# Value matmuls in blocks of eight key tiles instead of four, in a planned attention and feed-forward kernel

## The chip, the cores and the metric

The kernel runs on one core of a Trainium2 chip. The metric is the device time of one execution in microseconds, as the median of several runs. TensorE is called PE here, ScalarE ACT, VectorE DVE, GpSimd POOL and SyncE SP, as the profile does; PEld is PE's weight load.

## The reference

A layer norm without scale, then multi-query attention and a gated feed-forward block beside each other, all in fp32. The sequence has 2048 rows of width 448; there are 16 heads of width 28 that share one key and one value head; the feed-forward width is 1792.

```python
xn = _layernorm(x)
q = (xn @ wq).reshape(B, S, 16, 28).transpose(0, 2, 1, 3)
k, v = xn @ wk, xn @ wv
p = softmax(einsum("bhqd,bkd->bhqk", q, k) * 28 ** -0.5)
attn = einsum("bhqk,bkd->bhqd", p, v).transpose(0, 2, 1, 3).reshape(B, S, 448) @ wo
mlp = (silu(xn @ w1) * (xn @ w3)) @ w2
out = x + attn + mlp
```

## The kernel before

The 2048 query rows are taken in four chunks of 512 (`NQ`). A chunk of one head is called a head here: there are 64 (`NH`), numbered `h`, each against 16 key tiles of 128 rows (`KT`).

The work of a head:

- *Leads* (`leads`, matmul at L792, tile `ld`): the scores of all 16 key tiles, one 512-column matmul each. DVE takes the running maximum over them (`mx`, L803). ACT copies those of the key tiles that are kept, in neighbouring pairs, from PSUM to SBUF (`pa`, L797): five pairs for some heads (`TEN`), six for every second head from the twelfth on (`TWELVE`).
- The maximum over the keys, negated, is written to DRAM (`md`) and comes back as one row of the query stack (`qs`) and as a broadcast tile (`mb`).
- *Weights* (`weights_of`): for a kept pair POOL adds `mb` (L839, 128x1024) and ACT takes the exponential (L841). For the other tiles PE computes the score again, with the maximum as an extra row of the contraction (`sc`, L846), and ACT takes the exponential from PSUM (`pb`, L849).
- *Values* (`values`, L866): one matmul per key tile and head, with the 128x32 value tile as weights (28 columns, one column of ones for the sum of the softmax, padding) and the 128x512 exponentials as the moving operand, in plain fp32. Its output goes to one of four 32-column strips: the head's parity and the position's parity choose it. Each such matmul is two instructions.
- `pair_done` moves the sums of two heads from the bank `av` to `o` (ACT L881, DVE L882); after four heads `norm` divides and splits (POOL L914 and L918), and `out_project` multiplies with `wo`.

The values are issued in blocks. A block is one operation of the plan: it waits for all exponentials that it needs and issues its matmuls one after another. It takes `AVK` positions of head h (the first half of its order) and `AVK` positions of head h-1 (the second half):

```python
for i in range(AVK):
    for g, n in ((h, AVK * j + i), (h - 1, KT // 2 + AVK * j + i)):
        if 0 <= g < NH:
            todo.append((avb[g // 2], g, n, *pt[g, kept(g)[2][n]]))
...
cost = AVK / 2 * 858.0 + 300.0
plan.base = begin(h) + T * AVK * (j + 1) / KT + 1.5
```

The caller runs `j` over `range(KT // AVK // 2)`. With `AVK = 4` that is two blocks per head step of at most eight matmuls; h goes from 0 to 64, so there are 130 blocks, those of the first and the last step with one head only.

Beside this runs the feed-forward part (`hidden`): for each of 56 pieces (four chunks by 14) the chains `g` and `u` of 11 matmuls each (`gate_up`), a tanh on ACT (L686), two products on DVE (L688, L694), and a split into a high and a low part, ACT (L698) and POOL (L700, tile `h`); then `down`, chains `dn` whose results DVE adds to `acc` (L723). All matmuls of these chains and of the projections are written by `chain` (L409). In the first chunk the weights are loaded raw and split by ACT and POOL (L650, L652, L666, L668), stored, and reloaded for the later chunks. At the start come the norm, transposes (`xp`, L541) and the projections `q`.

The order on every engine is fixed when the program is built. `Plan.order` simulates the five engines with a cost for each operation and always issues the ready one with the lowest due time on each engine. The due times are made of `T0`, `T`, `LEAD`, `SPAN` (heads), `MDUE`, `MSTEP`, `MEND` (feed-forward), `XDUE`, `QDUE`, `QSTEP`, `XSTORE` (start, projections, stores) and a shift per kind of operation (`PUT`: engine and the buffers touched). An operation that needs new buffers is held back by `SOON` (how far ahead of PE's next due time it may go), `MOST` and `SPARE` (how many buffers a kind may hold, how many it must leave). Buffers come from three pools: single tiles of 2 KB per partition (`PAGES`, 18), double ones (`PAIRS`, 39) and the eight banks of PSUM. All DMAs are issued by SP. The value tiles use pairs (`pa`) and pages (`pb`).

Of the kernel before, what the change touches and what calls it, by code (L numbers as in the profile page):

```python
# [40 lines left out]
TWELVE = ((1, 4, 6, 9, 11, 14), (1, 0, 3, 2, 4, 5, 6, 7, 8, 9, 10, 11, 12, 13, 14, 15),  # L41
          (1, 2, 4, 5, 0, 6, 7, 9, 10, 3, 11, 12, 14, 15, 8, 13))
FROM, OF, MANY = 12, 2, 1
AVK = 4
T0, T, LEAD, SPAN = 73.28, 32.63, 14.04, 29.75
XDUE = (4.15, 8.15, 12.15, 16.15)
QDUE, QSTEP = 21.57, 6.09
SINGLE = 2
XSTORE = 22.5, 16.1
MDUE, MRUSH, MSTEP = 40, 11, 10.34  # L50
MEND = 7.58
RATE = 18.1
QUEUES = 16
LANES = 8
BACKLOG = 1565.91
LATE = 901.2
HLV = 0
EARLY = 16
BULK = ("w13", "w2", "x", "raw", "raw2", "acc")
SOON = {"pa": 30.2, "qs": 15.3, "acc": 15.9, "o": 18.3, "x": 24.2}  # L60

PUT = {"ACT ": -1.32, "ACT at pa": 0.93, "ACT at pb": -0.15, "ACT at x": 1.75, "ACT at xp": 8.68,
        "ACT av o": -9.5, "ACT h mi": -0.39, "ACT h t": -0.01, "ACT kv qp": -3.95, "ACT lb o oh": -0.08,
        "ACT mi t": -0.59, "ACT mi x": 2.0, "ACT o oh": 1.81, "ACT qp qt": -0.15, "ACT raw w13": -16.73,
        "ACT raw wo": 7.09, "DVE ": 1.37, "DVE acc": -5.45, "DVE acc xn": -2.36, "DVE at m": -0.89,
# [11 lines left out]
PAIRS = 39  # L77
PAGES = 96 - 2 * PAIRS
SLACK = 5.49
REST = 70.26  # L80
LOADING = 60
BANKS = 8
MOST = {"pa": 33, "x": 25, "acc": 10, "w13": 9, "w2": 8, "h": 3, "oh": 12, "wo": 4, "xt": 3, "xn": 1, "wq": 14,
        "qt": 4, "pb": 12, "raw": 4, "raw2": 5, "t": 2, "qs": 5, "m": 4, "mxt": 7, "mb": 7, "o": 19, "lb": 7,
        "xp": 33, "wr": 8, "kv": 7, "at": 5, "mi": 21, "av": 9, "qp": 14}
SPARE = {"x": 2, "acc": 4, "w13": 2, "w2": 4, "raw": 2, "raw2": 2, "qt": 6, "wo": 1, "qs": 2}


class Buf:
# [24 lines left out]
class Plan:  # L114
# [10 lines left out]
    def op(self, eng, cost, fn, reads=(), writes=(), parts=(), prio=0.0, after=(), lat=None, size=0, also=(), behind=None, k=16, port=False):  # L125
# [17 lines left out]
        o.bufs = list({id(b): b for b in bufs if b.ap is None}.values())  # L143
        o.prio += PUT.get(eng + " " + " ".join(sorted({b.cat for b in o.bufs})), 0.0)
        for b in o.bufs:
# [11 lines left out]
    def order(self):  # L157
        import heapq
        pools = list(range(PAGES)), list(range(PAIRS)), list(range(BANKS))
        pages, pairs, banks = pools  # L160
        used = dict.fromkeys(MOST, 0)
        ready = {e: [] for e in self.ENGINES}
# [13 lines left out]
        def head():  # L176

            while line and line[0][1] in issued:
                heapq.heappop(line)
            return line[0][0] if line else 1e9  # L180

        def can(o, early=False):
# [9 lines left out]
            if early:  # L192
                if any(len(p) - k < EARLY for k, p in zip(need[:2], pools) if k):
                    return False
            elif any(o.prio > head() + SOON.get(c, 40.0) for c in cats):
                return False
            if any(k > len(p) for k, p in zip(need, pools)):
                return False
            for c, k in cats.items():
                if used[c] + k > MOST[c] or len(pools[kinds[c]]) - need[kinds[c]] < SPARE.get(c, 0):  # L200
                    return False
# [16 lines left out]
        while todo:  # L218
            progress = True
            while progress:  # L220
                progress = False
                for e in self.ENGINES:
# [3 lines left out]
                    for o in ready[e]:  # L226
                        if best is not None and (o.prio, o.n) >= (best.prio, best.n):
                            continue
                        if e == "SP" and max(queues) - now > BACKLOG and o.prio > 40.0 and o.bufs and any(b.cat in BULK for b in o.bufs):
                            continue  # L230
# [114 lines left out]
def build(ctx, tc, x, wq, wk, wv, wo, w1, w3, w2, out):  # L345
# [208 lines left out]
    def x_store(qc):  # L554
        scr[qc] = dr.tile([7, P, TC], F32, tag=f"scr{qc}", name=f"scr{qc}")
        sbuf = fixed(scr[qc])
        store_ops[qc] = sbuf
        for c in range(7):
            b = xs[qc][c]
            dma(P * TC * 4, lambda b=b, c=c: nc.sync.dma_start(scr[qc][c], f32(b.ap)), reads=[b], parts=[sbuf])  # L560
# [34 lines left out]
    for qc in range(NQ):  # L595
        plan.base = XDUE[qc]
        norm_and_split(qc)
# [12 lines left out]
    for qc in range(1, NQ):  # L610
        plan.base = XSTORE[0] + XSTORE[1] * qc
        x_store(qc)
# [122 lines left out]
    def due(i):  # L735
# [3 lines left out]
        t = MDUE + MSTEP * MRUSH  # L739
        return t + (T0 + T * (NH + 1) / 2 + MEND - t) * (i - MRUSH) / (NQ * NF - MRUSH)  # L740

# [24 lines left out]
    def begin(h):  # L766

        return T0 + T / 2 * h
# [83 lines left out]
    def values(h, j):  # L852


        todo = []
# [7 lines left out]
        def fn():  # L863
            for a, g, n, p, i in todo:
                r = 64 * (n % 2) + 32 * (g % 2)
                nc.tensor.matmul(a.ap[r:r + 32], vst_ap[:, kept(g)[2][n]], p.ap if i is None else p.ap[:, i], start=(n < 2), stop=(n >= KT - 2),  # L866
                                 skip_group_check=True)
        cost = AVK / 2 * 858.0 + 300.0
        plan.base = begin(h) + T * AVK * (j + 1) / KT + 1.5
        av_last[0] = plan.op("PE", cost, fn, lat=cost + 160.0,  # L870
# [98 lines left out]
    for qc in range(NQ):  # L969
# [4 lines left out]
        for h in range(16 * qc, 16 * qc + (17 if qc == NQ - 1 else 16)):  # L974
            if h < NH:
                stack_load(h)
                leads(h)
            for j in range(KT // AVK // 2):
                for i in range(AVK * j, AVK * (j + 1)):
                    if h < NH:  # L980
# [17 lines left out]


# [17 lines left out]
```

## Time and profile before

| what | value |
|---|---|
| runs | 1123.69, 1124.69, 1121.7 us; median 1123.69 |
| profiled execution, first to last instruction (span) | 1120.7 us |
| PE busy | 1104.6 us, 5758 matmul instructions |
| PE weight loads busy | 736.5 us |
| POOL busy | 994.1 us, 499 instructions |
| ACT busy | 982.9 us, 1628 instructions |
| DVE busy | 946.0 us, 1802 instructions |
| DMA | 168.66 MB, 150 GB/s mean |
| mean granted TensorE clock | 0.997 |

The profiled execution is known by its span alone, so its own time is that span and what lies around it; the runs' times are 1.0 to 4.0 us above the span. Busy time of an engine is the union of its instructions' times. A matmul's row is longer than the distance to the next one, since matmuls are pipelined; the distance from start to start tells PE's pace. Rows of the timeline join neighbouring instructions of one kind (x3), with the start of the first.

### The profile page before, as it was taken

How to read it: one execution, taken by the hardware profiler on the slowest of the kernel's cores; microseconds unless marked ns; L12 is line 12 of the kernel's file. 1: busy time of each engine (PE TensorE's matmuls, PEld its weight loads, DVE VectorE, ACT ScalarE, POOL GpSimd, SP SyncE). 2: the span in 40 equal slices, each digit the busy share in tenths (PEclk: the TensorE clock that was granted, in tenths of full speed). 3: DMA queues.
4: the chain of work that ended last, by engine and by line, in shares of the span. 5: the costliest groups of instructions: out<-in, count | busy, mean ns of one | idle time of the engine just before them, and what ended most of it. 6: DMA issues, size and time to landing. Idle time of an engine off the chain costs nothing.

```text
span 1120.7 us, 18422 instructions
## 1 busy us (share of the span) xinstructions
PE 1104.6 (99%) x5758; PEld 736.5 (66%) x5758; DVE 946.0 (84%) x1802; ACT 982.9 (88%) x1628; POOL 994.1 (89%) x499
## 2 busy tenths in 40 slices
PE   6999999999999999999999999999999999999998
PEld 4877667666666676666666666666666676667664
DVE  7879776898898989899899888899889889898834
ACT  3466888999999989999899999999899989998962
POOL 3226999999999998999999998999989999999983
PEclk9999999999999999999999999999999999999999
DMA  6887777576425246242631461514452534335410
GB/s 180 264 264 257 254 255 255 159 227 214 164 62 155 69 135 207 59 140 75 232 124 50 148 224 53 166 45 156 142 173 75 174 127 150 102 92 161 142 56 33
DMA packets 99017, 168.66 MB, mean 150 GB/s; under 512 B 19804, under 2 KB 61468, under 8 KB 98920
## 3 DMA queue, kind: packets, MB, share of 16 engines
q1 hardware_dynamic: 98920, 167.50, 46.9%
q8 instruction: 45, 0.74, 0.3%
q14 instruction: 52, 0.43, 0.1%
HBM read 126.94 MB, written 39.83 MB: 149 GB/s over the span
## 4 chain that ended last, share of the span: by engine, by line
PE 94%; DVE 2%; ACT 2%; DMA 1%; issue 0%; SPq 0%; DVEq 0%; ACTq 0%
PE ld L792 22%; PE av L866 21%; PE g L409 12%; PE u L409 12%; PE dn L409 11%; PE sc L846 8%; PE q L409 4%; PE wo L409 3%; PE xp L541 1%; DVE mx L803 1%; ACT pa L841 1%; ACT pa L797 1%; DVE acc L723 1%; DMA acc<-x 0%; DVE sums L939 0%
## 5 line engine op out<-in xcount | busy, mean ns | idle before, releaser
L839 POOL TENSOR_TENSOR pa<-pa,mb 128x1024 f32<-128x1024 f32 x346 | 821.7, 2412 | 9.0 <-DMA mb<-md 6.4
L803 DVE TENSOR_TENSOR mx<-ld,mx 128x512 f32<-128x512 f32 x896 | 581.9, 682 | 73.0 <-PE ld L792 49.1
L797 ACT ACTIVATE pa<-ld 128x512 f32<-128x512 f32 x692 | 400.8, 622 | 39.7 <-PE ld L792 30.3
L841 ACT ACTIVATE pa<-pa 128x1024 f32<-128x1024 f32 x346 | 373.9, 1088 | 14.8 <-POOL pa L839 14.3
L792 PE MATMUL ld<-qs,kst 84*128 84x512 f32 x1024 | 351.4, 405 | 0.4 <-DVE mx L803 0.2
L792 PEld LDWEIGHTS ld<-qs,kst 84*128 84x128 f32 x1024 | 189.9, 189 | 100.8 <-DVE mx L803 21.6
L866 PE MATMUL av<-pa,vst 128*32 128x512 f32 x1384 | 248.3, 599 | 0.0
L866 PE MATMUL av<-pb,vst 128*32 128x512 f32 x664 | 245.6, 597 | 0.0
L849 ACT ACTIVATE pb<-sc 128x512 f32<-128x512 f32 x332 | 202.6, 617 | 17.3 <-PE sc L846 16.5
L409 PE MATMUL dn<-w,h 128*128 128x448 f32 x672 | 156.7, 368 | 0.0
L409 PEld LDWEIGHTS dn<-w,h 128*128 128x128 f32 x672 | 125.6, 188 | 23.3 <-issue 3.0
L846 PE MATMUL sc<-qs,kst 85*128 85x512 f32 x332 | 134.7, 410 | 0.0
L866 PEld LDWEIGHTS av<-pa,vst 128*32 128x32 f32 x1384 | 51.6, 109 | 91.7 <-issue 82.9
L700 POOL TENSOR_TENSOR h<-t,h 128x512 fp32r<-128x512 f32 x56 | 72.7, 1299 | 41.9 <-ACT h L698 40.6
L846 PEld LDWEIGHTS sc<-qs,kst 85*128 85x128 f32 x332 | 62.6, 188 | 45.7 <-DVE mx L803 11.1
L652 POOL TENSOR_TENSOR w<-raw,w 128x512 fp32r<-128x512 f32 x28 | 36.2, 1302 | 42.7 <-ACT w L650 25.2
L866 PEld LDWEIGHTS av<-pb,vst 128*32 128x32 f32 x664 | 48.1, 109 | 33.2 <-issue 33.2
L723 DVE TENSOR_TENSOR acc<-dn,acc 128x448 f32<-128x448 f32 x80 | 49.4, 618 | 23.0 <-PE dn L409 21.9
L409 PE MATMUL g<-x_0m,w 128*128 128x512 f32 x168 | 58.1, 396 | 0.0
L409 PE MATMUL g<-x_2m,w 128*128 128x512 f32 x168 | 56.6, 396 | 0.0
L409 PE MATMUL u<-x_2m,w 128*128 128x512 f32 x168 | 54.9, 393 | 0.0
L409 PE MATMUL u<-x_0m,w 128*128 128x512 f32 x168 | 54.9, 395 | 0.0
(85 smaller groups left out, 1187.0 us busy)
## 6 DMA issues: line engine op xcount, KB each, us to landing
w<-w13s SPq DMA_DIRECT2D x84, 512.0 KB
w<-w2s SPq DMA_DIRECT2D x42, 448.0 KB
mb<-md SPq DMA_DIRECT2D x64, 256.0 KB
w13s<-w SPq DMA_DIRECT2D x28, 512.0 KB
qs<-qd SPq DMA_DIRECT2D x64, 112.0 KB
wo<-wos SPq DMA_DIRECT2D x16, 448.0 KB
w2s<-w SPq DMA_DIRECT2D x14, 448.0 KB
raw<-w SPq DMA_DIRECT2D x28, 192.0 KB
```

The source lines that it names most:

```text
L409: nc.tensor.matmul(dst.ap[0:n, 0:width], lv(lb), rv(rb), start=(i == 0), stop=(i == len(terms) - 1))
L652: gps(512, lambda: nc.gpsimd.tensor_sub(l.ap, r.ap, f32(h.ap)), reads=[r, h], writes=[l], prio=-6.0)
L700: sub(512, lambda: eng.tensor_sub(hl.ap, p.ap, f32(hh.ap)), reads=[p, hh], writes=[hl], prio=2 * half)
L723: vec(448, lambda: nc.vector.tensor_add(a.ap[:, 0:D], o.ap[:, 0:D], a.ap[:, 0:D]), reads=[o, a], prio=1.0))
L792: last = pe(512, lambda m=m, kt=kt: nc.tensor.matmul(m.ap, kst_ap[0:KS, kt * P:(kt + 1) * P], q.ap[0:KS], start=True, stop=True), reads=[q ...
L797: act(512, lambda m=m, p=p, i=int(kt not in keeps): nc.scalar.activation(p.ap[:, i], m.ap, AF.Copy), reads=[m], parts=[p])
L803: vec(512, lambda m=m: nc.vector.tensor_max(mx.ap, m.ap, mx.ap), reads=[m], writes=[mx])
L839: gps(1024, lambda: nc.gpsimd.tensor_add(p.ap, p.ap, b.ap.unsqueeze(1).broadcast_to([P, 2, TC])), reads=[b], writes=[p], prio=-3.0)
L841: act(1024, lambda: nc.scalar.activation(p.ap, p.ap, AF.Exp, scale=SCALE), psum=False, writes=[p], prio=-1.0, after=[sqrt_last])
L846: pe(512, lambda: nc.tensor.matmul(o.ap, kst_ap[0:KS + 1, kt * P:(kt + 1) * P], q.ap[0:KS + 1], start=True, stop=True), reads=[q, kst[kt / ...
L849: act(512, lambda: nc.scalar.activation(p.ap, o.ap, AF.Exp, scale=SCALE), reads=[o], writes=[p], prio=0.0, after=[sqrt_last])
L866: nc.tensor.matmul(a.ap[r:r + 32], vst_ap[:, kept(g)[2][n]], p.ap if i is None else p.ap[:, i], start=(n < 2), stop=(n >= KT - 2), skip_gr ...
```

## The change

`AVK` becomes 8, so the caller makes one block per head step, 65 in all, of up to sixteen value matmuls (32 instructions). The kernel is built with `dynamic_dma_scratch_size=1024`. The buffers in SBUF grow from 96 pages' worth to 105: 42 pairs and 21 single tiles instead of 39 and 18. All numbers of the plan that set the order (due times, shifts, caps, spares) are new, so the order of the instructions on every engine is another one. No operation is added or removed.

```diff
-AVK = 4
-T0, T, LEAD, SPAN = 73.28, 32.63, 14.04, 29.75
-XDUE = (4.15, 8.15, 12.15, 16.15)
-QDUE, QSTEP = 21.57, 6.09
+AVK = 8
+T0, T, LEAD, SPAN = 72.48, 32.69, 13.9, 31.46
+XDUE = 2.98, 6.37, 17.56, 26.41
+QDUE, QSTEP = 25.9, 6.94
 SINGLE = 2
-XSTORE = 22.5, 16.1
-MDUE, MRUSH, MSTEP = 40, 11, 10.34
-MEND = 7.58
+XSTORE = 28.55, 18.09
+MDUE, MRUSH, MSTEP = 40.98, 11, 10.18
+MEND = 2.69
...
-BACKLOG = 1565.91
+BACKLOG = 1413
...
-EARLY = 16
+EARLY = 38
...
-SOON = {"pa": 30.2, "qs": 15.3, "acc": 15.9, "o": 18.3, "x": 24.2}
+SOON = {"acc": 21.59, "wr": 55.91, "xt": 40.28, "xn": 32.02, "mi": 40.31, "x": 19.15, "wq": 42.98, "qp": 42.98,
+        "qt": 11.86, "kv": 48.85, "at": 41.87, "xp": 44.05, "raw": 47.72, "wo": 45.16, "w13": 36.43,
+        "raw2": 51.69, "w2": 42.92, "t": 43.41, "h": 33.85, "qs": 12.37, "pa": 28.29, "m": 20.74, "mxt": 41.07,
+        "mb": 27.5, "pb": 44.78, "av": 11.92, "o": 2.37, "lb": 42.6, "oh": 39.42}
 
-PUT = {"ACT ": -1.32, "ACT at pa": 0.93, "ACT at pb": -0.15, "ACT at x": 1.75, "ACT at xp": 8.68,
...
+PUT = {"ACT ": 6.63, "ACT at pa": -0.43, "ACT at pb": -1.22, "ACT at x": -7.02, "ACT at xp": 14.58,
...
-PAIRS = 39
-PAGES = 96 - 2 * PAIRS
+PAIRS = 42
+PAGES = 105 - 2 * PAIRS
...
-MOST = {"pa": 33, "x": 25, "acc": 10, "w13": 9, "w2": 8, "h": 3, "oh": 12, "wo": 4, "xt": 3, "xn": 1, "wq": 14,
...
+MOST = {"acc": 10, "wr": 3, "xt": 3, "xn": 34, "mi": 29, "x": 19, "wq": 10, "qp": 20, "qt": 6, "kv": 5, "at": 5,
+        "xp": 40, "raw": 17, "wo": 23, "w13": 11, "raw2": 24, "w2": 6, "t": 4, "h": 3, "qs": 5, "pa": 50,
...
-    nc = _bacc.Bacc("TRN2", target_bir_lowering=False, num_devices=1)
+    nc = _bacc.Bacc("TRN2", target_bir_lowering=False, num_devices=1, dynamic_dma_scratch_size=1024)
```

More of the change, by code (lines that the diff above doesn't have):

```diff
@@ L54 @@
 LANES = 8
-BACKLOG = 1565.91
+BACKLOG = 1413
 LATE = 901.2
 HLV = 0
-EARLY = 16
+EARLY = 38
 BULK = ("w13", "w2", "x", "raw", "raw2", "acc")
-SOON = {"pa": 30.2, "qs": 15.3, "acc": 15.9, "o": 18.3, "x": 24.2}
-PUT = {"ACT ": -1.32, "ACT at pa": 0.93, "ACT at pb": -0.15, "ACT at x": 1.75, "ACT at xp": 8.68,
-        "ACT av o": -9.5, "ACT h mi": -0.39, "ACT h t": -0.01, "ACT kv qp": -3.95, "ACT lb o oh": -0.08,
-        "ACT mi t": -0.59, "ACT mi x": 2.0, "ACT o oh": 1.81, "ACT qp qt": -0.15, "ACT raw w13": -16.73,
-        "ACT raw wo": 7.09, "DVE ": 1.37, "DVE acc": -5.45, "DVE acc xn": -2.36, "DVE at m": -0.89,
[11 rows of a table removed]
-PAIRS = 39
-PAGES = 96 - 2 * PAIRS
+SOON = {"acc": 21.59, "wr": 55.91, "xt": 40.28, "xn": 32.02, "mi": 40.31, "x": 19.15, "wq": 42.98, "qp": 42.98,
[3 rows of a table added]
+PUT = {"ACT ": 6.63, "ACT at pa": -0.43, "ACT at pb": -1.22, "ACT at x": -7.02, "ACT at xp": 14.58,
+        "ACT av o": 0.5, "ACT h t": -2.71, "ACT kv qp": -11.23, "ACT mi t": -4.75, "ACT mi x": -22.23,
+        "ACT o oh": -16.42, "ACT pa": 3.47, "ACT qp qt": -14.01, "ACT raw w13": -8.51, "ACT raw wo": -5.69,
+        "ACT raw2 w2": 1.26, "ACT wq wr": 12.73, "DVE ": -2.76, "DVE acc": -22.01, "DVE acc mi": -3.14,
[6 rows of a table added]
+        "POOL mb pa": -2.4, "POOL o oh": -12.72, "POOL raw": -6.23, "POOL raw w13": -5.76,
[4 rows of a table added]
+PAIRS = 42
+PAGES = 105 - 2 * PAIRS
 SLACK = 5.49
@@ L82 @@
 BANKS = 8
-MOST = {"pa": 33, "x": 25, "acc": 10, "w13": 9, "w2": 8, "h": 3, "oh": 12, "wo": 4, "xt": 3, "xn": 1, "wq": 14,
-        "qt": 4, "pb": 12, "raw": 4, "raw2": 5, "t": 2, "qs": 5, "m": 4, "mxt": 7, "mb": 7, "o": 19, "lb": 7,
-        "xp": 33, "wr": 8, "kv": 7, "at": 5, "mi": 21, "av": 9, "qp": 14}
-SPARE = {"x": 2, "acc": 4, "w13": 2, "w2": 4, "raw": 2, "raw2": 2, "qt": 6, "wo": 1, "qs": 2}
+MOST = {"acc": 10, "wr": 3, "xt": 3, "xn": 34, "mi": 29, "x": 19, "wq": 10, "qp": 20, "qt": 6, "kv": 5, "at": 5,
+        "xp": 40, "raw": 17, "wo": 23, "w13": 11, "raw2": 24, "w2": 6, "t": 4, "h": 3, "qs": 5, "pa": 50,
+        "m": 5, "mxt": 11, "mb": 11, "pb": 15, "av": 8, "o": 15, "lb": 21, "oh": 20}
+SPARE = {"acc": 2, "wr": 5, "xt": 9, "xn": 5, "x": 4, "qp": 1, "qt": 6, "kv": 1, "xp": 4, "raw": 2, "w13": 3,
+        "raw2": 2, "w2": 5, "t": 2, "qs": 3, "m": 1, "mb": 2, "o": 5, "lb": 1, "oh": 1}
 class Buf:
```

21 rows, old and new, of the table PUT are left out of this document.

## The prediction

> **What bounds the kernel now.** I read the busy table first, then the table of stretches, then TensorE's (PE's) order of time around single value blocks, then the waits.
>
> ```profile
> PE 1104.6 (99%) x5758; PEld 736.5 (66%) x5758; DVE 946.0 (84%) x1802; ACT 982.9 (88%) x1628; POOL 994.1 (89%) x499
> ```
> ```profile
> core 0: us, PE busy (x) PEld busy (x) DVE busy (x) ACT busy (x) POOL busy (x), PEclk, DMA share, GB/s
> 0.00:40.00 40.00, 29.75 (x135) 22.96 (x136) 31.48 (x78) 15.59 (x31) 11.92 (x16) 0.96 0.71 203
> 40.00:120.00 80.00, 79.67 (x359) 61.44 (x357) 66.74 (x126) 52.86 (x94) 37.67 (x25) 1.00 0.80 264
> 120.00:400.00 280.00, 279.92 (x1472) 186.04 (x1471) 235.80 (x443) 259.51 (x435) 276.44 (x147) 1.00 0.54 176
> 400.00:1097.00 697.00, 697.00 (x3724) 454.87 (x3722) 600.84 (x1139) 650.72 (x1062) 662.96 (x308) 1.00 0.41 128
> 1097.00:1121.00 24.00, 18.22 (x78) 11.17 (x74) 11.14 (x19) 4.17 (x9) 5.15 (x7) 0.94 0.10 38
> ```
>
> The second fence is the kernel by stage. From 120 to 1097 us PE has work in 976.9 of 977 us at the full granted clock (1.00). Of the 16.1 us that PE lacks in the whole span (1120.7 - 1104.6), 10.6 lie before 120 us and 5.5 after 1097. GpSimd (POOL) comes next: 939.4 of the same 977 us (276.44 + 662.96), then ACT with 910.2 and DVE with 836.6. So a cut of PE's work shortens the run, as long as POOL can follow. PE's busy figure alone does not prove this, since matmul rows overlap; the distance from start to start does. Here is the first full value block and one near the end:
>
> ```profile
> 123.63 0.40 PE L792 MATMUL ld<-qs,kst 84*128 84x512 f32 x1
> 123.96 0.62 PE L866 MATMUL av<-pa,vst 128*32 128x512 f32 x1
> ...
> 125.82 0.51 PE L846 MATMUL sc<-qs,kst 85*128 85x512 f32 x1
> 126.16 0.64 PE L792 MATMUL ld<-qs,kst 84*128 84x512 f32 x2
> ```
> ```profile
> 633.53 0.40 PE L792 MATMUL ld<-qs,kst 84*128 84x512 f32 x1
> 633.76 0.39 PE L846 MATMUL sc<-qs,kst 85*128 85x512 f32 x1
> 633.99 0.40 PE L792 MATMUL ld<-qs,kst 84*128 84x512 f32 x1
> ```
> ```profile
> 1090.33 0.63 PE L846 MATMUL sc<-qs,kst 85*128 85x512 f32 x2
> 1090.88 0.63 PE L866 MATMUL av<-pa,vst 128*32 128x512 f32 x3
> ...
> 1091.34 0.61 PE L866 MATMUL av<-pa,vst 128*32 128x512 f32 x3
> ...
> 1091.77 0.61 PE L866 MATMUL av<-pa,vst 128*32 128x512 f32 x3
> ...
> 1092.20 0.61 PE L866 MATMUL av<-pa,vst 128*32 128x512 f32 x3
> 1092.74 0.50 PE L846 MATMUL sc<-qs,kst 85*128 85x512 f32 x1
> 1093.08 0.39 PE L409 MATMUL g<-x_0m,w 128*128 128x512 f32 x1
> ```
> ```profile
> 120.00:1097.00 977.00, 241.98 (x2016) 52.57 (x2016) 1.00 0.45 142
> ```
>
> Away from blocks a 512-column matmul starts 0.23 to 0.235 us after the one before (633.53, 633.76, 633.99). In a block four matmuls run side by side, one in each 32-column strip, and such rounds start at 1090.88, 1091.34, 1091.77 and 1092.20: 0.43 us each. A block of four key tiles for each of two heads is eight matmuls, sixteen instructions, four rounds, so its own work is 4 x 0.43 = 1.72. But from 1090.33 to 1093.08 pass 2.75 us, holding three ordinary matmuls (3 x 0.235 = 0.70) and the block: 2.75 - 0.70 - 1.72 = 0.33. The early block, from 123.63 to 126.16 with two ordinary matmuls: 2.53 - 0.47 - 1.72 = 0.34. Going into and out of a block costs 0.33 us, split between the wait before the first round, the last round's tail, and the slow first ordinary matmul after it. The last fence is the value matmuls' line in the long stretch: 2016 instructions, 126 blocks of sixteen. With the two half-filled blocks at each end that makes 130.
>
> **The change, part by part.**
>
> *Blocks of eight.* The loop over j runs once per head step instead of twice, so 130 blocks become 65. Matmuls, weight loads and rounds are the same in number: a long block is eight rounds, 3.44 us, with one entry and one exit. Removed: 65 x 0.33 = 21.45 us of PE time. Since PE has no other gap between 120 and 1097, all of this is on the path: 1120.7 - 21.45 = 1099.25. Bounds: nothing, if the 0.33 came per four tiles and not per block (the rounds inside show none of it, so I don't take it), and 65 x 0.34 = 22.1.
>
> *What waits longer.* A block starts when the exponentials of eight tiles of each head are there, and its first matmul holds up everything behind it in PE's queue: leads (ld), recomputed scores (sc), the feed-forward matmuls. Before 1097 PE waits at no block, and if the planner places blocks as late as now, it needs more weights held ready. By the order list a long block gathers about 5 pairs (pa) and 6 pages (pb) of the two heads, a short one 3 and 3. The diff adds 3 pairs (39 to 42) and 3 pages (18 to 21). That covers it. Cost nothing; without the room, each block that waited 0.33 us would give back its own saving.
>
> *The scratch.* The queue table has all data on the queue that SP fills:
>
> ```profile
> q1 hardware_dynamic: 98920, 167.50, 46.9%
> ```
>
> GpSimd issues no DMA, so a smaller scratch for DMAs that it would issue changes no instruction. Nothing either way; it makes room for the six extra buffers.
>
> *POOL's pace.* The stretch of 977 us loses 63 of the 65 entries, 20.8 us, and becomes 956.2. POOL's work in it stays 939.4: 98.2% busy where it is 96.2% now. This is the term that can cost. Its waits there:
>
> ```profile
> POOL h L700 <- ACT h L698: 20.9, 19, 2.9
> POOL oh L918 <- ACT oh L917: 6.9, 6, 2.2
> POOL pa L839 <- DMA mb<-md: 5.8, 4, 3.3
> POOL pa L839 <- DVE mx L803: 2.5, 1, 2.5
> ```
>
> POOL takes its queue in order, and these are a queue that had run ahead of ACT and DMA. A POOL that lags waits less: from 120 to 400 it worked 276.44 of 280 us, 98.7%, with PE full. Lower bound 0 (98.2% or more). Upper bound: the present 96.2% throughout, 20.8 us, the whole gain. I take 98%, near the row where POOL was pressed, a little below because some of the 19 waits for ACT stay: 939.4 / 0.98 = 958.6, that is +2.4. The waiting PE work would be the next value block.
>
> *The longer block and the evacuation engines.* For 3.44 + 0.33 = 3.8 us (now 2.05) no new scores reach PSUM. DVE and ACT live from the filled banks, at most five for leads and scores.
>
> ```profile
> L803 DVE TENSOR_TENSOR mx<-ld,mx 128x512 f32<-128x512 f32 x896 | 581.9, 682 | 73.0 <-PE ld L792 49.1 <-ACT pa L797 10.5 <-PE g L409 0.5
> L841 ACT ACTIVATE pa<-pa 128x1024 f32<-128x1024 f32 x346 | 373.9, 1088 | 14.8 <-POOL pa L839 14.3
> ```
>
> Five maxima at 0.68 are 3.4 us for DVE, and ACT has 346 exponentials of 1.09 us that need no PSUM, 5.4 per head. DVE idles 140.4 of the 977 us, ACT 66.8: per long block 2.2 and 1.06 us. An estimate of the starvation is under 0.5 us a block (3.8 - 3.4), inside both. Cost nothing as long as it stays there; beyond, it is the slow rival below.
>
> *The new order.* Priorities, due times and caps change which ready instruction goes first, and the queues of SP, POOL, ACT and DVE are all refilled in another order. Work and transfers stay the same in number. At the start, the quarters 2 and 3 of the input are due later (12.15 and 16.15 become 17.56 and 26.41), the first two slightly earlier; PE idles 10.25 us before 40 and 0.33 from there to 120, so it can lose or win a few us there. At the end, PE's last gaps (5.5 us) belong to the last head's normalisation in four slices. The last block grows by four rounds, 1.7 us; now a chain of u matmuls (1101.30 on) stands between the last exponential and the last block, so this hides, and costs 1.7 at most if that chain moves. Between -3 and +3 for both together; I take 0.
>
> ```profile
> 1097.78 1.06 ACT L841 ACTIVATE pa<-pa 128x1024 f32<-128x1024 f32 x1 [0.65 <-POOL pa L839]
> 1101.30 0.62 PE L409 MATMUL u<-x_0m,w 128*128 128x512 f32 x2
> 1103.88 1.05 PE L866 MATMUL av<-pa,vst 128*32 128x512 f32 x4
> ```
>
> *Sum.* 1120.7 - 21.45 + 2.4 = 1101.65 of span. The profiled execution's span lies 3.0 under the median of the runs (1123.69; they go from 1121.7 to 1124.69), and I carry that over: 1104.6.
>
> **The rivals.**
>
> *POOL becomes the bound.* If it keeps 3% idle, the stretch takes 939.4 / 0.97 = 968.5 and 8.5 us are left of the gain: 1115. At 2.5% it is 963.5, saved 13.5: 1110. For it: the later 697 us run at 95.1%, and each wait for ACT stops everything behind it. Against: the 98.7% of the 280 us before. The Trainium skill (Perfetto Trace Analysis, Identifying the Most-Contended Engine) says to look for the engine with the highest occupancy and not to judge TensorE by matmul busy time but by weight loads. By that rule POOL (89%) stands above PE's loads (66%) and a cut on PE buys little; the trace disagrees in so far as matmul starts follow each other without a gap, while POOL has 37.6 us of idle in the stretch.
>
> *The entry cost isn't saved.* If the new order breaks the eight tiles' work up again, or PE waits 0.33 us at each long block for the last exponential, time stays: 1121 to 1126. For it: long blocks need twice the weights at one moment. Against: six more buffers, and no wait at blocks now. The Trainium skill (TensorEngine Tiling, Key Properties) states that changing the tiling mode, not merely the tile, drains TensorE. By that rule the cost belongs to the switch; the rounds inside the block, at 0.43 throughout, agree.
>
> *Slower: the long block starves ACT.* It decides from 1.06 us of ACT idle per long block on, since 910.2 + 63 x 1.06 = 977. At 1.3 us it would be 910.2 + 81.9 = 992.1, 15 more than now: 1139. For it: ACT is 93% busy (910.2 of 977) and reads every kept lead and every recomputed score from PSUM. Against: short blocks cost it little so far, as its waits for leads and scores show over the whole run:
>
> ```profile
> ACT pa L797 <- PE ld L792: 30.3, 43, 3.4
> ACT pb L849 <- PE sc L846: 16.5, 27, 1.9
> ```
>
> *More than the sum.* The new order also fills part of PE's 16.1 us of idle at the ends and POOL costs nothing: 1104.6 - 2.4 - 4 = 1098.
>
> **How the numbers follow.** Forecast, gain nearly whole (1100.5 to 1107.5): 0.56. POOL as the bound (1107.5 to 1120): 0.22. Entry cost not saved: 0.07. Slower: 0.08. More: 0.07. So faster 0.56 + 0.22 + 0.07 = 0.85, same 0.07, slower 0.08, where 0.3% (3.4 us) is about what a measurement of this kernel can tell from no change. From 1098.5 to 1116 lie the forecast, most of POOL's case and half of the last one, 0.8 in all.
>
> **What would show it.** In the profile of the changed kernel: 2048 value instructions in 65 blocks, each with eight rounds 0.43 apart and one 0.33 around them; PE again without gaps from 120 us to about 24 us before the end; POOL at 98% or more between, with its waits for ACT's h well under 20.9 us. POOL's case shows as PE gaps ahead of value blocks released by ACT's pa exponentials, those in turn by POOL; the slow case as longer ACT waits for ld and sc. The forecast is wrong if rounds inside a block lose their 0.43, if PE stands at blocks, or if the start loses more than 3 us to the later input quarters.

## The result and the profile after

The changed kernel takes 1104.7 us (median; 1103.79 to 1105.64) against 1123.56 for the kernel before on the same chip: a ratio of 0.9832, 95% interval 0.982 to 0.9844. The forecast was 1104.6. The span of the profiled execution went from 1120.7 to 1102.3 us. The busy table after:

```profile
PE 1083.5 (98%) x5758; PEld 747.6 (68%) x5758; DVE 948.9 (86%) x1802; ACT 976.9 (89%) x1628; POOL 994.5 (90%) x499
```

Every count of instructions is the same as before, and PE's busy time has fallen by 21.1 us. By stage (columns: stretch, its length, busy time and instructions of PE, PEld, DVE, ACT, POOL, then clock, DMA share and GB/s):

```profile
0.00:40.00 40.00, 26.77 (x123) 20.32 (x123) 32.38 (x73) 16.14 (x32) 13.31 (x17) 1.00 0.73 209
40.00:120.00 80.00, 79.00 (x356) 61.61 (x357) 69.31 (x132) 53.77 (x95) 36.41 (x23) 1.00 0.74 238
120.00:400.00 280.00, 280.00 (x1496) 193.63 (x1496) 238.26 (x445) 260.41 (x439) 278.83 (x148) 1.00 0.56 184
400.00:1077.00 677.00, 677.00 (x3681) 460.00 (x3680) 597.73 (x1135) 641.05 (x1057) 658.32 (x307) 1.00 0.41 131
1077.00:1103.00 26.00, 20.74 (x106) 11.99 (x104) 11.21 (x19) 5.50 (x10) 7.66 (x7) 0.99 0.10 36
```

From 120 to 1077 us PE is full again, and POOL works 937.15 of 957 us, 97.9%. But in the first 120 us PE has done 105.77 us of work where it had done 109.42, so the start lost 3.65 us. One long block in PE's order of time (rows left out at the dots), and the line of the value matmuls between 120 and 1077 us:

```profile
603.48 0.40 PE L850 MATMUL sc<-qs,kst 85*128 85x512 f32 x1
603.81 0.63 PE L870 MATMUL av<-pa,vst 128*32 128x512 f32 x3
...
604.26 0.60 PE L870 MATMUL av<-pa,vst 128*32 128x512 f32 x3
...
606.42 0.59 PE L870 MATMUL av<-pa,vst 128*32 128x512 f32 x1
...
606.84 0.59 PE L870 MATMUL av<-pa,vst 128*32 128x512 f32 x1
...
607.38 1.42 PE L796 MATMUL ld<-qs,kst 84*128 84x512 f32 x5
608.64 0.57 PE L413 MATMUL dn<-w,h 128*128 128x448 f32 x2
```
```profile
120.00:1077.00 957.00, 225.70 (x1984) 58.08 (x1984) 1.00 0.45 147
```

The 1984 instructions are 62 blocks of 32. The eight rounds run from 603.81 to 606.84 at 0.43 us each, with nothing extra where two short blocks would have met. From 603.48 to 608.64 there are six ordinary matmuls and eight rounds: 5.16 - 6 x 0.235 - 8 x 0.43 = 0.31, one entry and exit for twice the work. (Going into and out of a block is called an entry here for short.)

### The profile page after: what moved, and what is told of

Its sections match the earlier page's. It is cut to its first block, busy times and chain, and to the rows that moved or that the text cites. A ratio compares the mean times of both kernels' runs of the same rounds, so it can differ in the third digit from the quotient of the medians.

```text
span 1102.3 us, 18349 instructions
## 1 busy us (share of the span) xinstructions
PE 1083.5 (98%) x5758; PEld 747.6 (68%) x5758; DVE 948.9 (86%) x1802; ACT 976.9 (89%) x1628; POOL 994.5 (90%) x499
## 4 chain that ended last, share of the span: by engine, by line
PE 95%; DVE 3%; DMA 0%; issue 0%; ACT 0%; SPq 0%; DVEq 0%
PE ld L796 22%; PE av L870 21%; PE g L413 13%; PE u L413 13%; PE dn L413 12%; PE sc L850 7%; PE wo L413 3%; PE q L413 2%; DVE xn L532 1%; PE xp L545 0%; DVE xn L535 0%; DVE acc L727 0%; DMA acc<-x 0%; DVE sums L943 0%; DVE x L552 0%; DVE st L511 0%
## 5 line engine op out<-in xcount | busy, mean ns | idle before, releaser
L807 DVE TENSOR_TENSOR mx<-ld,mx 128x512 f32<-128x512 f32 x896 | 578.6, 683 | 56.1 <-PE ld L796 29.7
L870 PE MATMUL av<-pa,vst 128*32 128x512 f32 x1384 | 235.3, 596 | 0.0
L870 PE MATMUL av<-pb,vst 128*32 128x512 f32 x664 | 233.4, 594 | 0.0
L853 ACT ACTIVATE pb<-sc 128x512 f32<-128x512 f32 x332 | 207.5, 631 | 10.7 <-PE sc L850 9.7
L413 PE MATMUL dn<-w,h 128*128 128x448 f32 x672 | 172.3, 368 | 0.7 <-POOL h L704 0.7
L850 PE MATMUL sc<-qs,kst 85*128 85x512 f32 x332 | 131.8, 402 | 0.0
L870 PEld LDWEIGHTS av<-pa,vst 128*32 128x32 f32 x1384 | 58.1, 109 | 100.6 <-issue 92.1
L870 PEld LDWEIGHTS av<-pb,vst 128*32 128x32 f32 x664 | 53.4, 110 | 39.3 <-issue 39.3
L413 PE MATMUL u<-x_2m,w 128*128 128x512 f32 x168 | 59.0, 395 | 0.0
L413 PE MATMUL u<-x_0m,w 128*128 128x512 f32 x168 | 58.6, 395 | 0.0
```

The costliest lines, as they stand in the source:

```text
L413: nc.tensor.matmul(dst.ap[0:n, 0:width], lv(lb), rv(rb), start=(i == 0), stop=(i == len(terms) - 1))
L807: vec(512, lambda m=m: nc.vector.tensor_max(mx.ap, m.ap, mx.ap), reads=[m], writes=[mx])
L850: pe(512, lambda: nc.tensor.matmul(o.ap, kst_ap[0:KS + 1, kt * P:(kt + 1) * P], q.ap[0:KS + 1], start=True, stop=True), reads=[q, kst[kt / ...
L853: act(512, lambda: nc.scalar.activation(p.ap, o.ap, AF.Exp, scale=SCALE), reads=[o], writes=[p], prio=0.0, after=[sqrt_last])
```

## Experiments

Three questions: is the gain the entries that went away, is the rest of the change (order, room, scratch) needed, and what would have been the next bound.

**Is it the entry into the block? One extra matmul, at the edge or in the middle.** Both kernels add one matmul with zero weights per full block and plan it with the same cost; only its place differs. In the two traces DVE, ACT and POOL go through their work in the same order. The edits, shortened:

```diff
 for a, g, n, p, i in todo:
+    # e2: here, before the ninth of sixteen
+    # nc.tensor.matmul(avb[(h - 1) // 2].ap[0:112], zero_ap, kst_ap[:, 0:TC], start=False, ...)
     nc.tensor.matmul(a.ap[r:r + 32], vst_ap[...], p..., ...)
+# e1: here, after the last
```

> The changed kernel with one extra matmul right after each of the 63 full blocks: 112 columns of zeros as weights, 512 columns moving, float32r, added onto the value bank, so it adds zero. It stands beside ordinary matmuls, so no new entry into or exit from a block. Entry theory (0.33 us for each entry and exit of a block, PE the bound): 63 x 0.235 = 14.8 us more, 1119.5. POOL theory (PE has room, POOL sets the pace): clearly under 1112.

> The same extra matmul with the same planned cost, but in the middle of each full block, between its fourth and fifth round, so each block is left and entered once more. Entry theory: 14.8 + 63 x 0.33 = 35.6 us over the changed kernel, 1140.3, that is 20.8 over the run with the matmul at the end. Rival (the 0.33 belongs to the block's start, a wait for its exponentials or its weights, and not to the change between the two kinds of matmul): the same time as with the matmul at the end, about 1119.5.

Measured: 1124.84 at the edge (ratio to before 1.0011, 1.0002 to 1.0021) and 1143.94 in the middle (1.0184, 1.0163 to 1.0205): 19.1 us apart where 63 x 0.33 = 20.8 were expected. PE's order of time at the end of a block with the matmul at the edge, then with it in the middle:

```profile
613.60 0.59 PE L873 MATMUL av<-pb,vst 128*32 128x512 f32 x1
614.12 0.49 PE L876 MATMUL av<-kst,zero 128*112 128x512 f32 x1
614.45 0.36 PE L414 MATMUL dn<-w,h 128*128 128x448 f32 x1
614.65 1.31 PE L799 MATMUL ld<-qs,kst 84*128 84x512 f32 x5
```
```profile
623.76 0.60 PE L876 MATMUL av<-pa,vst 128*32 128x512 f32 x3
...
624.19 0.60 PE L876 MATMUL av<-pa,vst 128*32 128x512 f32 x3
624.73 0.49 PE L873 MATMUL av<-kst,zero 128*112 128x512 f32 x1
625.15 0.62 PE L876 MATMUL av<-pa,vst 128*32 128x512 f32 x2
```

At the edge the extra matmul (614.12) takes the place of the slow first ordinary one, and the next two start 0.33 and 0.20 us later, so it costs about an ordinary matmul. In the middle the next round starts at 625.15, 0.96 us after the last (624.19) where rounds are otherwise 0.43 apart: 0.53 more, of which 0.235 is an ordinary matmul and 0.30 the change there and back. The cost belongs to the switch between value matmuls and ordinary ones, not to a wait for the block's data.

The two kinds differ in two things, the 32-column strips and the number format (plain fp32 in the values, float32r in the others; the profile prints f32 for both), and the extra matmul changes both. No run parts them. The kernel before has plain fp32 transposes over the whole array (`xp`) between float32r matmuls:

```profile
37.03 0.85 PE L409 MATMUL q<-x,wq 128*126 128x512 f32 x3
37.72 1.03 PE L541 MATMUL xp<-ident,xn 128*128 128x128 f32 x8
38.51 0.47 PE L409 MATMUL g<-x,w 128*128 128x512 f32 x1
38.83 0.39 PE L792 MATMUL ld<-qs,kst 84*128 84x512 f32 x1
```

The transposes start 0.69 us after the first `q`, three ordinary steps of 0.23. From 37.72 to 38.83 are 1.11 us: eight transposes at 0.109 and one ordinary matmul at 0.235 are 1.11, with nothing left for a switch. So the format alone seems to cost nothing, which speaks for the strips; but a transpose is one instruction and a value matmul two, so it does not settle it.

At the edge the time missed by 5 us (1124.84, 1119.5 expected). The planner, given another cost, made another order: DVE and ACT go through their work differently than in the changed kernel. Counted over all of PE's starts from the first block to the last, what the steps between ordinary matmuls are too long (those more than 0.04 us over the usual 0.235, or 0.206 for 448 columns; the one right after a block left out) adds up to 7.9 us of waits here and to 1.3 in the changed kernel, which covers the 5 us. The next runs show how much that can be.

**The new order without the long block, and the long block without the new order.**

```diff
-AVK = 8        (changed kernel, e3)
+AVK = 4
-AVK = 4        (kernel before, with 42 pairs, 21 pages, small scratch, e4)
+AVK = 8
```

> The changed kernel with all its new numbers and buffers, planned for blocks of four key tiles. Entry theory: 65 entries more, 1104.7 + 21.5 = 1126. Order theory (the new due times and buffers made the gain, the block length is by the way): about 1105, under 1112.

> The kernel before with its own due times, caps and shifts, with blocks of eight, 42 pairs, 21 pages and the small scratch. Entry theory: 1123.6 - 21.5 = 1102, up to 1107 if the old due times leave PE standing at some blocks. Order theory: about 1123.

Measured: 1134.2 (1.0089, 1.0072 to 1.0106) and 1146.05 (1.0188, 1.0166 to 1.021). The first refutes the order theory: without long blocks the new numbers give no gain at all. It is 8 us worse than the entries alone explain; PE's waits, counted as above, are 9.2 us instead of 1.3. That the due times were not found for short blocks is the likely reason, and not shown. The second is a clear miss of mine: with long blocks in the old order the kernel is 1.9% slower than before, not 2% faster. Waits of DVE, POOL and PE's weight loads between 120 and 1077 us there (us in total, times, longest), and then DVE's in the changed kernel:

```profile
DVE mx L803 <- PE ld L792: 70.9, 59, 4.5
```
```profile
POOL pa L839 <- DMA mb<-md: 22.8, 7, 6.3
```
```profile
PEld ld L792 <- DVE mx L803: 16.8, 44, 1.2
```
```profile
DVE mx L807 <- PE ld L796: 29.7, 53, 1.5
```

With the old due times DVE ran dry for leads, up to 4.5 us at a time, and elsewhere PE's leads waited for DVE's maxima (16.8 us; the same row of the changed kernel has 1.3). The long block is part of it: of the 73.7 us that the maxima waited for leads (both lines of `mx` together), about 44 lie beside a value block on PE, and 3.6 of the longest 4.5; in the changed kernel it is 4 of 31.5. POOL waited 22.8 us for the broadcast of the maximum, 5.8 before the change. PE's instructions between 120 and 1077 us tell the loss, in this run, before the change and after it:

```profile
120.00:1077.00 957.00, 942.42 (x4971) 621.29 (x4970) 812.40 (x1545) 874.85 (x1448) 895.85 (x433) 0.99 0.45 143
120.00:1077.00 957.00, 956.92 (x5081) 627.50 (x5079) 830.25 (x1570) 898.03 (x1480) 919.40 (x445) 1.00 0.45 145
120.00:1077.00 957.00, 957.00 (x5175) 653.63 (x5175) 835.99 (x1579) 901.46 (x1495) 937.15 (x454) 1.00 0.45 147
```

The old order with long blocks gets 110 instructions less far than the kernel before, the changed kernel 94 further. PE's waits, counted as above, are 38 us between ordinary matmuls and 3 in or before blocks, which covers what this profiled run's span is above the changed kernel's (1139.6 - 1102.3 = 37.3). How they divide among DVE, ACT, POOL and the granted clock (0.99 here) is not shown.

**Which part of the new order matters.**

```diff
 (e4, with)
+T0, T, LEAD, SPAN, XDUE, QDUE, QSTEP, XSTORE, MDUE, MSTEP, MEND, PUT of the changed kernel
 (EARLY, SOON, MOST, SPARE, BACKLOG stay old)
```

> The run with the old numbers, blocks of eight and the new room, which took 1146, with the new due times and shifts (T0 to MEND, XDUE, QDUE, XSTORE, PUT) put in, the caps (EARLY, SOON, MOST, SPARE, BACKLOG) still old. If the old due times were what left PE and DVE standing there: 1105 to 1125, most of the 41 us to the changed kernel back. If the caps were: over 1135.

Measured: 1113.3 (0.9921, 0.9904 to 0.9937). The due times and shifts bring back 32.8 of the 41.4 us, and the new caps on top of them the other 8.6. The new caps with the old due times were not run. Its first 120 us:

```profile
0.00:40.00 40.00, 29.32 (x136) 23.21 (x137) 31.70 (x78) 16.59 (x34) 13.51 (x17) 1.00 0.71 201
40.00:120.00 80.00, 79.73 (x359) 62.16 (x358) 69.75 (x132) 54.48 (x98) 36.20 (x23) 1.00 0.78 256
```

PE does 109.05 us here, as before the change, with the new due times of the input quarters. So the 3.65 us lost at the start come with the new caps. The other traces agree: PE does 105.1 to 106.4 us in the first 120 in every run with the new caps, and 109.0 to 110.2 in every run with the old ones.

**Room and scratch.**

```diff
-PAIRS = 42, PAGES = 105 - 2 * PAIRS, dynamic_dma_scratch_size=1024      (changed kernel, e5)
+PAIRS = 39, PAGES = 96 - 2 * PAIRS
+dynamic_dma_scratch_size=1024                                          (kernel before, e9: this alone)
+PAIRS = 42, PAGES = 105 - 2 * PAIRS, dynamic_dma_scratch_size=1024      (kernel before, e10)
```

> The changed kernel with its new due times, shifts and caps, blocks of eight, but the buffers of before: 39 pairs, 18 pages, the default scratch. Theory that the block's gathering needs the six buffers: the planner must delay exponentials, PE or POOL stands at many blocks; a block that waits 0.33 us loses its own saving, so from 1125 up, with POOL's idle time well over the 20 us of the changed kernel. Rival (room is by the way): 1104 to 1110.

> The kernel before with dynamic_dma_scratch_size=1024 and nothing else; the order and the buffers stay. Theory that nothing uses that scratch: 1123.6, ratio 1.000. Rival (the smaller scratch moves something, in the launch or the addresses): a difference over 0.3%.

> The kernel before, blocks of four, with 42 pairs, 21 pages and the small scratch; the planner may use the six buffers. Entry theory: no entry goes away, so nothing is gained: 1120 to 1128. Room theory (more buffers feed the engines better whatever the block): under 1115.

Measured: 1160.99 (1.0345, 1.0326 to 1.0365), 1122.96 (1.0001, 0.9992 to 1.0011) and 1124.26 (1.0018, 1.0009 to 1.0028). The scratch moves nothing, and room alone gives short blocks nothing. But without the room the changed kernel loses 56 us: in its stretch from 120 to 1077 us PE gets through 4863 instructions instead of 5175 and POOL works only 890.7 us.

```profile
120.00:1077.00 957.00, 938.64 (x4863) 616.11 (x4862) 807.34 (x1518) 859.30 (x1423) 890.70 (x432) 0.98 0.43 138
```

The loss isn't spread evenly over the blocks. Most of it lies in the first 180 us of the stretch, where the weights of the feed-forward part are still being prepared; first without the room, then the changed kernel:

```profile
120.00:300.00 180.00, 165.31 (x757) 102.59 (x756) 109.70 (x200) 133.25 (x220) 158.21 (x93) 0.91 0.59 194
120.00:300.00 180.00, 180.00 (x951) 127.37 (x951) 146.96 (x271) 162.20 (x276) 179.73 (x103) 1.00 0.71 236
```

Of the 312 instructions that PE is behind, 194 are lost here, and the granted clock is 0.91. Over the whole run PE's waits, counted as above, are 42 us between ordinary matmuls and 13 in or before blocks. How much of this is the lower clock is not shown.

**Does POOL's 98% cost anything?** Both kernels keep the changed kernel's order on every engine and alter only POOL's additions: e6 leaves out 128 of 1024 columns of each, e7 adds a small second one for each head.

```diff
-nc.gpsimd.tensor_add(p.ap, p.ap, b.ap...)                      (e6)
+nc.gpsimd.tensor_add(p.ap[:, :, 0:448], p.ap[:, :, 0:448], b.ap[:, 0:448]...)
+if kt == keeps[0]:                                             (e7, after the full addition)
+    nc.gpsimd.tensor_add(p.ap[:, :, 0:32], p.ap[:, :, 0:32], b.ap[:, 0:32]...)
```

> The changed kernel in the same order on every engine, but POOL adds the maximum to 896 instead of 1024 columns of each kept pair (the other columns are left without it, so the weights of those queries are not the reference's): about 0.29 us less for each of 346 additions, 100 us of POOL's time. Prediction's term (POOL at 98% costs PE 2.4 us): 1102.3. Rival (PE alone sets the time, POOL costs it nothing): 1104.7.

> The changed kernel in the same order, but POOL does a second, small addition of 64 columns on the first kept pair of each head (the maximum is subtracted twice there, so those weights are not the reference's): about 0.25 us for each of 64 heads, 16 us more for POOL, which has some 20 us of idle time between 120 and 1077 us. Theory that PE is the bound and POOL's idle time is usable slack: 1104.7 to 1108. Theory that POOL is the next bound already: nearer to 1104.7 + 16 = 1121.

Measured: 1104.54 (0.9838, 0.9824 to 0.9853) and 1115.97 (0.9941, 0.9926 to 0.9956). The busy tables of the two, and POOL's waits for ACT's h between 120 and 1090 us in the second:

```profile
PE 1084.9 (98%) x5758; PEld 748.7 (68%) x5758; DVE 948.3 (86%) x1802; ACT 976.5 (89%) x1628; POOL 900.1 (82%) x499
```
```profile
PE 1092.5 (98%) x5758; PEld 741.4 (67%) x5758; DVE 950.0 (85%) x1802; ACT 975.9 (88%) x1628; POOL 1014.3 (91%) x563
```
```profile
POOL h L704 <- ACT h L702: 5.7, 6, 1.3
```

94.4 us less of POOL's work change the time by 0.2 us, well inside the interval: POOL costs the changed kernel nothing. 19.8 us more (0.31 for each small addition, not 0.25) cost 11.3, between the two expectations: of POOL's 20 us of idle time about 8.5 could be used, 0.9% of the stretch. So PE sets the time of the changed kernel, and POOL is close behind. Two things stay open: the small additions all sit on the first kept pair of a head, so part of the 11.3 can come from that pair's later exponential and not from POOL's total; and whether ACT or DVE has less to spare was not tried.

## Why the prediction was right

*The entries.* 65 x 0.33 = 21.45 us was the main term; PE's busy time fell by 21.1, the blocks show one entry each, and the pair of runs with the extra matmul isolates 0.30 us per switch, by time (19.1 / 63, where the intervals of the two runs allow 0.04 either way) and by the rows. PE's waits outside the blocks did not change (1.0 us before, 1.3 after, counted as above), so the gain in the stretch is not a better order in disguise. The Trainium skill (TensorEngine Tiling (Array Packing), Key Properties) says that a change of tiling mode drains TensorE; the trace shows a cost at each change between value and ordinary matmuls, 0.30 to 0.33 us, but not that it is a drain.

*POOL at 98%.* The share came as said (97.9%), but its price of 2.4 us is the step that failed: the run with 94 us less of POOL's work shows a price of 0. POOL's waits for ACT's h were to fall well under 20.9 us and fell to 16.6; those for the broadcast `mb`, 5.8 us before, are gone from the stretch.

*The new order.* Set to 0 between -3 and +3, it was +2.65: 3.65 lost at the start, 1.0 won at the end, where PE now lacks 4.5 us (25.27 - 20.74) and lacked 5.5. So 1120.7 - 21.1 + 2.65 = 1102.25, the measured span; busy and idle time always make up the span, so this shows where the time went and not why. The two errors, +2.4 for POOL and 0 for the order, cancelled by luck; the total was better than its parts. A start that loses more than 3 us to the later input quarters was named as a sign against the forecast. It lost 3.65, but the named cause wasn't right: the new due times leave the start as it was (e8), the new caps with them do not. At the start PE's transposes now wait for the normalised input more often and 3.3 us longer, before and after:

```profile
PE xp L541 <- DVE xn L528: 8.6, 1, 8.6
```
```profile
PE xp L545 <- DVE xn L532: 11.9, 8, 8.5
```

*The room.* Right that three pairs and three pages cover the gathering: no block of the changed kernel waits. The price of its absence was far too low: each waiting block would give back its own 0.33, I said, 21 us in all; it was 56. Nor was it mainly the blocks that stood: PE lost most of it between ordinary matmuls and in the first 180 us of the stretch, and POOL did 890.7 us of work instead of 937.15.

*The long block and the evacuation engines.* Nothing in the changed kernel: DVE's waits for leads between 120 and 1077 us fell from 48.2 us to 29.7. But I took that as a property of the block, and it is one of the order. The mechanism of the slow rival exists, in DVE more than in ACT (ACT's waits for leads are 22.9 us in the old order and 18.8 in the changed kernel): under the old numbers DVE stands beside the long blocks, in a run that is 41 us slower. How much of the 41 us it costs is not shown. It stayed away here because a new order came with the change.

*The 3.0 us* between span and median were 2.4 this time (1104.7 - 1102.3).

*The rule on occupancy.* By the Trainium skill (Perfetto Trace Analysis, Identifying the Most-Contended Engine) POOL, at 90% busy against 68% of weight loads, would be the engine to relieve. (The section names a second measure for TensorE, MFU, the share of its peak arithmetic; it was not worked out here.) The run that relieves POOL by 94 us gains nothing; here the distance between matmul starts was the better guide.

## What to carry to other kernels

When an engine sets the time, count its transitions as well as its work: read the step from start to start inside a run of equal instructions, subtract it from the stretch around the run, and multiply what is left by the number of runs. Merging runs needs buffers for what must be gathered and an order that feeds the other engines through the longer run; with either missing this merge turned a gain of 1.7% into a loss of 1.9 to 3.5%. Test the price of a nearly full engine by making its work shorter in the same order before you optimise it.

## What the runs showed of the hardware

The cost of a switch shows partly one matmul later: the first ordinary start comes 0.54 us after the last round (606.84 to 607.38) instead of 0.43, and the start after that 0.33 instead of 0.235, even where it is a matmul put there for nothing (614.12 to 614.45). And PE's busy time can hide waits: with the same 5758 matmuls it was 1083.5 us in the changed kernel and 1092.5 with the slower POOL, because a matmul's row (0.40 us) is longer than the step to the next (0.235) and covers waits under 0.17 us. Instructions per stretch, and the steps from start to start, told the loss where busy time did not.
